# First layer's weights: the shift of the low word on ScalarE, the subtraction for the low part on VectorE

## The chip, the cores and the metric

The kernel runs on one core of a Trainium2 chip. The time is that of the device for one execution, in microseconds (us); less is better. The engines are named as in the profile: PE is TensorE's matmul, PEld its weight load, DVE is VectorE, ACT is ScalarE, POOL is GpSimd, SP is SyncE, which issues all the DMAs.

## The reference

Attention first: 4 batches, 8 heads of 64, 512 local and 32 global positions. Global queries see every key; a local query sees the global keys and the local ones within 32 positions of it. The result, 2176 tokens by 512, goes through two feed-forward layers, each with weights of its own (512 by 2048 and 2048 by 512):

```python
def _moe_ref(x, w_in, w_out):
    h = x @ w_in
    g = h * (1.0 / (1.0 + np.exp(-h)))
    return (g @ w_out).astype(np.float32)

def _moe2_ref(x, w_in, w_out):
    h = x @ w_in
    g = h * np.cos(h)
    return (g @ w_out).astype(np.float32)
```

Queries, keys and values are float32. The four weight matrices are float64, and they reach the chip as pairs of 32-bit words.

## The kernel before, in words

**Precision.** TensorE multiplies in a rounded float32 format (`F32R` in the code). So each operand is split into a high part, which is the value rounded to that format, and a low part, which is the value minus the high part. Each product is then three matmuls: low by high, high by high and high by low.

**Tiles and slots.** The tokens are cut into 8 tiles of 256 (the last has 384), the 2048 hidden units into 16 blocks of 128. A *slot* is one block of hidden units of one tile of tokens: `gemm1` (12 matmuls, L426 to L428) fills a PSUM tile `ps_hid`, ACT and DVE make the nonlinearity of it (`silu`, L434 and L435, in the first layer), `split_g` makes the two parts of the result (the cast `gh` on ACT, L406; the subtraction `gl`, L407, which is on POOL for the first layer's tiles 0 and 1 and on DVE elsewhere), and two slots later `gemm2` (12 matmuls, L493 to L495) adds it to the output tile `ps_y`. `ps_hid` has two buffers in the first layer, so `gemm1` of a slot waits for DVE's `silu` of the slot two before.

**Order.** The attention of tiles 0 and 1 comes before slot 0. Then the first layer's tiles 0 and 1 run with their slots in turn (slots 0 to 31), while the attention of tile 2 and the first global queries are spread between them. From slot 32 on the other tiles follow, then the second layer. Up to slot 40 the order of the instructions on every engine is left to the framework's scheduler, which sorts them by priority and by its own idea of when each is ready; from slot 40 it is the order written in the plan. Every engine works off its own queue in order.

**The first layer's weights.** They come as 32 chunks (`f` from 0 to 15, `part` 0 for `w_in`, 1 for `w_out`) of 128 rows by 512 float64 numbers, so 128 by 1024 words, and a chunk is needed at about one per slot. A chunk goes through these steps, planned in slots that follow one another:

- `load_w1` (SP, L99): one DMA of 512 KB into the tile `raw`, which has a buffer of its own for each chunk.
- `rebias` (ACT, L109): scales the high words, seen as float32, in place, which puts the exponent right.
- `to_f32` (DVE): shifts the low words right by 29, in place (L115); puts the sign bit of the high word to it (L116); shifts the high word left by 3 and joins the two (L120). The result is the chunk as float32, `w`, in a staging pool of three buffers that other tiles use too.
- `split_w`: the high part by a cast on ACT (L140), or on POOL for the first three chunks (L138, `POOLED`); the low part by a subtraction on POOL (L141). Both are written to `wt`, in the place where `raw` was.

The second layer's weights (`ph` of 1) are turned to float32 by the same functions in chunks of half the size, from slot 32 on, stored, and loaded and split when the second layer begins.

Of the kernel before, what the change touches and what calls it, by code (L numbers as in the profile page):

```python
# [11 lines left out]
F32 = mybir.dt.float32  # L12
F32R = mybir.dt.float32r
I32 = mybir.dt.int32
AF = mybir.ActivationFunctionType
ALU = mybir.AluOpType
PSUM = bass.MemoryType.PSUM
# [22 lines left out]
ROUND = 12582912.0  # L40
REBIAS = 2.0**-112
SIGN = -(2**31)


@with_exitstack
def attention_then_two_ffn(
# [9 lines left out]
    nc = tc.nc  # L56
# [32 lines left out]
    tiles = [(t, SPAN if t < NB - 1 else SPAN + B * SG) for t in range(NB)]  # L89
    x1 = [dram.tile([128, NP, n], F32, name=f"x1_{t}") for t, n in tiles]  # L90

# [1 line left out]
    w2f = [[dram.tile([128, 512], F32, name=f"w2f_{f}_{part}") for part in range(2)] for f in range(NF)]  # L93
    wh, wl = {}, {}
    W = {}

    def load_w1(f, part):
        raw = wts.tile([128, 1024], I32, tag=f"w{part}_{f}", name="raw")
        nc.sync.dma_start(out=raw, in_=w1[f, :, part * 1024 : part * 1024 + 1024])  # L99
        W[0, f, part] = raw.rearrange("p (n two) -> p n two", two=2)  # L100

    def load_w2_words(f, part):
        raw = stage.tile([128, 512], I32, tag="r", bufs=3, name="raw")
        nc.sync.dma_start(out=raw, in_=w2[f, :, part * 512 : part * 512 + 512])
        W[1, f, part] = raw.rearrange("p (n two) -> p n two", two=2)

    def rebias(ph, f, part):
        high = W[ph, f, part][:, :, 1].bitcast(F32)
        nc.scalar.activation(out=high, in_=high, func=AF.Copy, scale=REBIAS)  # L109

    def to_f32(ph, f, part):
        words = W[ph, f, part]
        n = words.shape[1]
        low, high = words[:, :, 0], words[:, :, 1]
        nc.vector.tensor_scalar(out=low, in0=low, scalar1=29, scalar2=None, op0=ALU.logical_shift_right)  # L115
        nc.vector.scalar_tensor_tensor(  # L116
            out=low, in0=high, scalar=SIGN, in1=low, op0=ALU.bitwise_and, op1=ALU.bitwise_or
        )
        w = stage.tile([128, n], F32, tag="f", name="w")
        nc.vector.scalar_tensor_tensor(  # L120
            out=w.bitcast(I32), in0=high, scalar=3, in1=low, op0=ALU.logical_shift_left, op1=ALU.bitwise_or
        )
        W[ph, f, part] = w
# [9 lines left out]
    def split_w(ph, f, part):  # L133
        w = W.pop((ph, f, part))
        t = wts.tile([128, 1024], F32R, tag=f"w{part}_{f}", name="wt")
        hi, lo = t[:, 0:512], t[:, 512:1024]
        if ph == 0 and 2 * f + part < POOLED:
            nc.gpsimd.tensor_scalar(out=hi, in0=w, scalar1=1.0, scalar2=1.0, op0=ALU.mult, op1=ALU.mult)  # L138
        else:
            nc.scalar.copy(hi, w)  # L140
        nc.gpsimd.tensor_tensor(out=lo, in0=w, in1=hi.bitcast(F32), op=ALU.subtract)  # L141
        wh[ph, f, part], wl[ph, f, part] = hi, lo

# [1 line left out]
    def attention_pools(stack):  # L145
        for name, bufs in (("qk", 2), ("v", 2), ("gin", 1), ("s", 2), ("t1", 1), ("st", 4)):
            P[name] = stack.enter_context(tc.tile_pool(name=name, bufs=bufs))

    # global values: rows hold [hi, lo, hi]; zeros between the two heads of a pair
    def load_vg(b):  # L150
        raw = stage.tile([128, DM], F32, tag="f", name="vraw")
        nc.sync.dma_start(out=raw[0:96], in_=vg3[b])
        t = P["t1"].tile([96, NP, 3, D], F32R, tag="vst", name="vst")
        nc.gpsimd.memset(t[:, :, 1, :].bitcast(F32), 0.0)
        vst[b] = t, raw
# [7 lines left out]
        )  # L163
        vst[b] = t.rearrange("r p h d -> r p (h d)")

    # P of the global keys, transposed: rows hold its parts [hi, hi, lo]
    def glob_keys_t(p, blocks):
        tg = P["t1"].tile([SG, blocks, 128], F32, tag="tg", name="tg")
        for g in range(4):
            rows = slice(32 * g, 32 * g + 32)  # L170
            nc.vector.transpose(out=tg[:, :, rows], in_=p[rows])
        return tg
# [5 lines left out]
        nc.gpsimd.tensor_tensor(out=pgt[64:96], in0=tg, in1=pgt[0:32].bitcast(F32), op=ALU.subtract)  # L178
        return pgt

    # local queries: four blocks of 64 queries, two heads each
    def load_qk(n):
        t = P["qk"].tile([128, QKCOLS], F32, tag="qk", name="qk")
        nc.sync.dma_start(out=t, in_=units[n, :, 0:QKCOLS])
        q = t[:, 0 : UNIT * 128].rearrange("p (c x) -> p c x", c=UNIT)
        k = t[:, UNIT * 128 : QKCOLS].rearrange("p (c x) -> p c x", c=UNIT)
        A[n] = {"q": q, "k": k}
# [31 lines left out]
    def unit_exp(n):  # L219
        s, st = A[n]["s"], A[n]["st"]  # L220
        for j in range(UNIT):
            nc.scalar.activation(
                out=s[:, j, :], in_=s[:, j, :], func=AF.Exp, bias=st[:, j : j + 1], scale=-1.0,
                accum_out=st[:, UNIT + j : UNIT + j + 1],
# [73 lines left out]
            nc.vector.tensor_tensor(out=lo, in0=po, in1=hi.bitcast(F32), op=ALU.subtract)  # L298
            A.pop(n)

    # global queries: 32 queries of four heads over all keys
    def load_glob_qk(n):
        t = P["gin"].tile([128, 2, 64 + KG], F32, tag="gin", name="gin")
        for i in range(2):
            nc.sync.dma_start(out=t[:, i, :], in_=glob[2 * n + i, :, 0 : 64 + KG])
        G[n] = {"qk": t}
# [27 lines left out]
    def glob_exp(n):  # L334
        st = G[n]["st"]
        G[n]["s"] = s = P["s"].tile([128, KG], F32, tag="s", name="sg")
        for c, ps in enumerate(G[n].pop("ps")):
            nc.scalar.activation(
                out=s[:, c * KG // 2 : (c + 1) * KG // 2], in_=ps, func=AF.Exp, bias=st[:, 2:3], scale=SCALE,
                accum_out=st[:, 3 + c : 4 + c],  # L340
# [54 lines left out]
            nc.vector.tensor_tensor(out=lo, in0=po, in1=hi.bitcast(F32), op=ALU.subtract)  # L395
            G.pop(n)

# [1 line left out]
    widest = [max(n for t, n in tiles if t % 3 == i) for i in range(3)]  # L399
    xbuf = [[xp.tile([128, NP, w], F32R, name=f"x{part}{i}") for part in "hl"] for i, w in enumerate(widest)]  # L400

# [29 lines left out]
    def silu(t, f):  # L431
        h = H.pop((0, t, f))
        a = M["a"].tile([128, tiles[t][1]], F32, tag="a", name="act")
        nc.scalar.activation(out=a, in_=h, func=AF.Tanh, scale=0.5)  # L434
        nc.vector.scalar_tensor_tensor(out=a, in0=a, scalar=1.0, in1=h, op0=ALU.add, op1=ALU.mult)  # L435
        g32[0, t, f] = a

    def turns(t, f):
# [3 lines left out]
        r = M["a"].tile([128, n], F32, tag="a", name="rest")  # L442
        nc.scalar.activation(out=k, in_=h, func=AF.Copy, scale=INV_TWO_PI, bias=ROUND)  # L443
        nc.vector.tensor_scalar(out=k, in0=k, scalar1=-ROUND, scalar2=None, op0=ALU.add)  # L444
# [4 lines left out]
    def load_sine():  # L449
        nc.scalar.activation(out=half_pi_sine, in_=half_pi, func=AF.Sin)  # L450

# [70 lines left out]
                r0 = t * SPAN + i * 128  # L522
                nc.sync.dma_start(out=out[r0 : r0 + 128, :], in_=o)

# [1 line left out]
    P, M, A, G, X1, H, Y, gq, g32, vst = ({} for _ in range(10))  # L526
    LAG = (2, 4)
    EARLY = 2 * NP
# [7 lines left out]
    last = (NB - 1) * NF  # L536
# [3 lines left out]
    def at(rank, i, fn, *args):  # L540
        plan.setdefault(i, []).append((rank, fn, args))
# [46 lines left out]
        if n + 1 < 2 * B:  # L588
            at(post, s + 5, load_glob_qk, n + 1)

    # attention of the first two tiles, then that of each later one during the tile before
    for n in range(2 * NP):
        plan_early_unit(n, n - LEAD)
    plan_glob(0, G0)
# [5 lines left out]
    for t in range(3, NB):  # L600
        s = (t - 1) * NF
# [7 lines left out]
        if t % 2 == 0:  # L609
            at(post, s - 2, load_vg, t // 2)  # L610
            at(pre, s + 2, split_vg, t // 2)
    # weights of the first layer
    chunks = sorted((seq.index((0, 0, f)) + LAG[0] * part, f, part) for f in range(NF) for part in range(2))
    s = len(seq)
    for need, f, part in reversed(chunks):
        s = max(min(s - 1, need - SLACK), 2 - LEAD)
        at(post, max(s - LOADS, 1 - LEAD), load_w1, f, part)
        at(pre, s, rebias, 0, f, part)
        at(pre, s + 1, to_f32, 0, f, part)
        at(pre, s + 2, split_w, 0, f, part)  # L620
    # weights of the second layer: to float32 meanwhile, to their place after the last use of the first's
    for i in range(4 * NF):
        s = PAIR + i * (last - PAIR - 4) // (4 * NF)
        at(post, s - 2, load_w2_words, i // 4, i % 4)
        at(pre, s, rebias, 1, i // 4, i % 4)
        at(pre, s + 1, to_f32, 1, i // 4, i % 4)
        at(pre, s + 1, store_w2, i // 4, i % 4)
    for f in range(NF):
        for part in range(2):
            s = last + f + 1 + part * LAG[0]  # L630
            at(post, s - 1, load_w2, f, part)
            at(pre, s, split_w, 1, f, part)
    # the two layers
    at(pre, last + NF, load_sine)
    for i, (ph, t, f) in enumerate(seq):
        at(pre, i + 1 + 2 * ph, split_g, ph, t, f)
# [8 lines left out]
    for t in range(NB):  # L645
        s = last + t * NF
# [97 lines left out]
```

## Time and profile before

| | |
|---|---|
| time, median of 3 runs | 947.88 us (947.23 to 948.92) |
| span of the profiled execution | 945.8 us |
| median less span, taken as what lies around the span | 2.1 us |
| PE busy | 908.6 us, 96% of the span |
| DVE busy | 666.3 us, 70% |
| ACT busy | 506.9 us, 54% |
| POOL busy | 185.9 us, 20% |
| chain that ended last | PE 86%, DVE 9%, DMA 2%, ACT 1% |

The profile is of one execution. Of the profiled execution its span is given; its own time is taken as the span and the 2.1 us beside it. Busy shares are means over a kernel whose parts differ: PE's 96% holds stretches with no idle time and one, early, in which it stands still again and again, so the shares have to be read by stretch.

### The profile page before, as it was taken

The page shows a single profiled execution, that of the slowest core. Times are in us where ns is not written, and L with a number is a line of the kernel's source. Part 1 is how long each engine was busy: PE and PEld are TensorE (multiplying, and loading weights), DVE is VectorE, ACT ScalarE, POOL GpSimd, SP SyncE. Part 2 cuts the span into 40 slices and gives each one's busy share as a digit, 9 for nine tenths or more (in the row PEclk, how much of TensorE's full clock was granted, in tenths as well). Part 3 has the DMA queues.
Part 4 walks back from the last instruction along what each step waited for, and adds up shares of the span by engine and source line. Part 5 has one row for each costly group of instructions (what it writes and reads, how often), then busy time and mean ns, then how long its engine had stood idle before and what let it go on. Part 6 is the DMA issues. An engine that isn't in the chain of part 4 may idle for free.

```text
span 945.8 us, 18534 instructions
## 1 busy us (share of the span) xinstructions
PE 908.6 (96%) x6800; PEld 851.0 (90%) x6800; DVE 666.3 (70%) x1873; ACT 506.9 (54%) x1386; POOL 185.9 (20%) x205
## 2 busy tenths in 40 slices
PE   6987889999999999999999999999999999999998
PEld 5676778999999999999999999999999999999997
DVE  5999995567686868778753557666666666676664
ACT  5655554445454545545445566565555555555543
POOL 2566664301111111110115650000000000000000
PEclk9998878999999999999999999999999999999999
DMA  8876421264464655656305440101010101010000
GB/s 284 301 246 221 167 93 37 74 206 158 157 218 147 193 184 158 190 164 192 116 29 167 128 140 2 45 1 45 1 46 1 45 1 45 2 56 1 23 1 33
DMA packets 48203, 102.12 MB, mean 108 GB/s; under 512 B 5361, under 2 KB 14065, under 8 KB 48113
## 3 DMA queue, kind: packets, MB, share of 16 engines
q1 hardware_dynamic: 48112, 100.95, 33.1%
q8 instruction: 53, 0.87, 0.4%
q14 instruction: 38, 0.30, 0.1%
HBM read 83.62 MB, written 17.30 MB: 107 GB/s over the span
## 4 chain that ended last, share of the span: by engine, by line
PE 86%; DVE 9%; DMA 2%; ACT 1%; issue 1%; SPq 0%; POOL 0%; ACTq 0%; DVEq 0%
PE ps_hid L428 13%; PE ps_hid L427 13%; PE ps_hid L426 13%; PE ps_y L493 7%; PE ps_y L500 7%; PE ps_y L499 7%; PE ps_y L501 7%; PE ps_y L495 6%; PE ps_y L494 6%; PE ps_s L200 3%; DVE w L120 2%; DVE raw L115 2%; DVE raw L116 2%; PE ps_o L286 2%; DMA raw<-in_w_dram 1%; PE ps_t L264 1%
## 5 line engine op out<-in xcount | busy, mean ns | idle before, releaser
L426 PE MATMUL ps_hid<-xh,wt 128*128 128x256 f32 (+1 forms) x1024 | 298.7, 292 | 10.2 <-DVE act L435 5.9
L427 PE MATMUL ps_hid<-xh,wt 128*128 128x256 f32 (+1 forms) x1024 | 298.1, 291 | 0.0
L428 PE MATMUL ps_hid<-xl,wt 128*128 128x256 f32 (+1 forms) x1024 | 298.1, 291 | 0.0
L426 PEld LDWEIGHTS ps_hid<-xh,wt 128*128 128x128 f32 x1024 | 197.6, 193 | 17.0 <-DVE act L435 6.5
L427 PEld LDWEIGHTS ps_hid<-xh,wt 128*128 128x128 f32 x1024 | 197.5, 193 | 4.9
L428 PEld LDWEIGHTS ps_hid<-xl,wt 128*128 128x128 f32 x1024 | 197.3, 193 | 0.0
L493 PE MATMUL ps_y<-gh,wt 128*128 128x256 f32 (+1 forms) x512 | 157.5, 308 | 0.0
L495 PE MATMUL ps_y<-gl,wt 128*128 128x256 f32 (+1 forms) x512 | 150.5, 294 | 0.5 <-POOL gl L407 0.5
L494 PE MATMUL ps_y<-gh,wt 128*128 128x256 f32 (+1 forms) x512 | 150.1, 293 | 0.0
L443 ACT ACTIVATE turns<-ps_hid 128x256 f32<-128x256 f32 (+1 forms) x128 | 50.8, 397 | 154.5 <-PE ps_hid L428 154.5
L444 DVE TENSOR_SCALAR turns<-turns 128x256 f32<-128x256 f32 (+1 forms) x128 | 38.7, 302 | 111.1 <-ACT turns L443 111.1
L500 PE MATMUL ps_y<-wt,gh 128*128 128x512 f32 x272 | 107.4, 395 | 0.0
L407 DVE TENSOR_TENSOR gl<-act,gh 128x256 fp32r<-128x256 f32 (+1 forms) x96 | 49.3, 513 | 82.4 <-ACT gh L406 82.2
L499 PE MATMUL ps_y<-wt,gl 128*128 128x512 f32 x272 | 107.2, 394 | 0.0
L501 PE MATMUL ps_y<-wt,gh 128*128 128x512 f32 x272 | 106.1, 390 | 0.0
L493 PEld LDWEIGHTS ps_y<-gh,wt 128*128 128x128 f32 x512 | 99.5, 194 | 4.6 <-issue 2.5
L495 PEld LDWEIGHTS ps_y<-gl,wt 128*128 128x128 f32 x512 | 99.7, 195 | 1.1 <-POOL gl L407 0.7
L494 PEld LDWEIGHTS ps_y<-gh,wt 128*128 128x128 f32 x512 | 99.9, 195 | 0.4 <-issue 0.4
L141 POOL TENSOR_TENSOR wt<-w,wt 128x512 fp32r<-128x512 f32 x64 | 89.8, 1415 | 51.8 <-ACT wt L140 46.6
L434 ACT ACTIVATE act<-ps_hid 128x256 f32<-128x256 f32 (+1 forms) x128 | 50.3, 393 | 53.8 <-PE ps_hid L428 52.7
L406 ACT CAST gh<-act 128x256 fp32r<-128x256 f32 (+1 forms) x128 | 52.9, 413 | 45.5 <-DVE act L435 22.0
L109 ACT ACTIVATE raw<-raw 128x256 f32<-128x256 f32 (+1 forms) x96 | 49.7, 519 | 51.0 <-DMA raw<-in_w_dram 50.9
(88 smaller groups left out, 1532.0 us busy)
## 6 DMA issues: line engine op xcount, KB each, us to landing
qk<-in_units_dram SPq DMA_DIRECT2D x32, 576.0 KB, 4.1
raw<-in_w_dram SPq DMA_DIRECT2D x32, 512.0 KB, 7.8
raw<-in_w_dram SPq DMA_DIRECT2D x64, 256.0 KB, 3.7
v<-in_units_dram SPq DMA_DIRECT2D x32, 256.0 KB, 3.0
w2f<-w SPq DMA_DIRECT2D x64, 128.0 KB, 1.8
w<-w2f SPq DMA_DIRECT2D x32, 256.0 KB, 2.6
gin<-in_glob_dram SPq DMA_DIRECT2D x16, 304.0 KB, 3.2
out_dram<-y SPq DMA_DIRECT2D x17, 256.0 KB, 2.1
```

The costliest lines, as they stand in the source:

```text
L141: nc.gpsimd.tensor_tensor(out=lo, in0=w, in1=hi.bitcast(F32), op=ALU.subtract)
L406: nc.scalar.copy(hi, src)
L426: nc.tensor.matmul(h, lo[:, ws], xh[:, k, :], start=k == 0, stop=False)
L427: nc.tensor.matmul(h, hi[:, ws], xh[:, k, :], start=False, stop=False)
L428: nc.tensor.matmul(h, hi[:, ws], xl[:, k, :], start=False, stop=k == NP - 1)
L443: nc.scalar.activation(out=k, in_=h, func=AF.Copy, scale=INV_TWO_PI, bias=ROUND)
L493: nc.tensor.matmul(o, lo[:, ds_], gh, start=first, stop=False, skip_group_check=True)
L494: nc.tensor.matmul(o, hi[:, ds_], gh, start=False, stop=False, skip_group_check=True)
L495: nc.tensor.matmul(o, hi[:, ds_], gl, start=False, stop=f == NF - 1, skip_group_check=True)
L499: nc.tensor.matmul(y[c], gl[:, cs], hi, start=f == 0, stop=False)
L500: nc.tensor.matmul(y[c], gh[:, cs], hi, start=False, stop=False)
L501: nc.tensor.matmul(y[c], gh[:, cs], lo, start=False, stop=f == NF - 1)
```

## The change

Three edits, all for the first layer's weights (`ph` of 0), and the two constants that one of them needs:

- `rebias` also does the shift of the low words, on ACT. A second activation reads the word as an unsigned integer, scales it by 2^-29 (a little less), adds a bias of almost -0.5, and writes it back as an integer, rounded, which gives the three bits that the shift gives.
- `to_f32` leaves out the shift on DVE (L115).
- `split_w` makes the low part on DVE, not on POOL (L141).

For the second layer's weights all stays as it was.

```diff
+U32 = mybir.dt.uint32
+TOP3 = 2.0**-29 * (1.0 - 2.0**-18)
+TOP3_BIAS = -0.5 + 7.5 * 2.0**-18
...
     def rebias(ph, f, part):
         high = W[ph, f, part][:, :, 1].bitcast(F32)
         nc.scalar.activation(out=high, in_=high, func=AF.Copy, scale=REBIAS)
+        if ph == 0:
+            low = W[ph, f, part][:, :, 0]
+            nc.scalar.activation(out=low, in_=low.bitcast(U32), func=AF.Copy, scale=TOP3, bias=TOP3_BIAS)
...
         low, high = words[:, :, 0], words[:, :, 1]
-        nc.vector.tensor_scalar(out=low, in0=low, scalar1=29, scalar2=None, op0=ALU.logical_shift_right)
+        if ph == 1:
+            nc.vector.tensor_scalar(out=low, in0=low, scalar1=29, scalar2=None, op0=ALU.logical_shift_right)
...
-        nc.gpsimd.tensor_tensor(out=lo, in0=w, in1=hi.bitcast(F32), op=ALU.subtract)
+        sub = nc.vector if ph == 0 else nc.gpsimd
+        sub.tensor_tensor(out=lo, in0=w, in1=hi.bitcast(F32), op=ALU.subtract)
```

## Rows read from the trace of the kernel before

**Rows 1.** Busy time of each engine by stretch (stretch, its length, then busy us)

```profile
core 0: us, PE busy (x) PEld busy (x) DVE busy (x) ACT busy (x) POOL busy (x), PEclk, DMA share, GB/s
...
25.00:43.00 18.00, 16.59 (x139) 12.18 (x139) 16.14 (x64) 12.75 (x43) 9.23 (x19) 1.00 0.89 298
43.00:150.00 107.00, 84.69 (x658) 79.53 (x654) 106.01 (x176) 57.31 (x138) 69.02 (x61) 0.89 0.53 178
150.00:190.00 40.00, 39.73 (x344) 38.98 (x345) 18.78 (x68) 18.16 (x56) 14.47 (x18) 0.96 0.18 57
...
230.00:500.00 270.00, 270.00 (x2496) 262.94 (x2496) 201.82 (x687) 135.62 (x422) 39.73 (x48) 1.00 0.51 160
```

**Rows 2.** Chain that ended last, 43 to 150 us, shares by line

```profile
by line: DVE w L120 19.8%; DVE raw L115 19.4%; DVE raw L116 17.8%; issue 10.0%; DMA raw<-in_w_dram 4.2%; DVE act L435 3.5%; DVE s L233 2.7%; DVE tg L171 2.5%; DVE sg L349 1.8%; DVE s L212 1.7%; DVE stg L329 1.4%; PE ps_y L495 1.2%; PE ps_y 
```

**Rows 3.** DVE's groups, 43 to 150 us (count, busy us, mean ns, idle before)

```profile
L116 DVE SCALAR_TENSOR_TENSOR raw<-raw 128x512 int32<-128x512 int32 x28 | 29.3, 1066 | 0.2
L115 DVE TENSOR_SCALAR raw<-raw 128x512 int32<-128x512 int32 x28 | 27.9, 1027 | 0.1
L120 DVE SCALAR_TENSOR_TENSOR w<-raw 128x512 int32<-128x512 int32 x28 | 24.7, 896 | 0.1
L435 DVE SCALAR_TENSOR_TENSOR act<-act,ps_hid 128x256 f32<-128x256 f32 x21 | 8.6, 408 | 0.0
L233 DVE TENSOR_SCALAR s<-s,st 128x160 f32<-128x160 f32 x8 | 5.6, 746 | 0.0
```

**Rows 4.** Timeline of DVE and of POOL, 79 to 86 us (start, length)

```profile
82.54 0.41 DVE L115 TENSOR_SCALAR raw<-raw 128x512 int32<-128x512 int32 x1
83.06 0.69 DVE L116 SCALAR_TENSOR_TENSOR raw<-raw 128x512 int32<-128x512 int32 x1
...
85.99 0.67 DVE L120 SCALAR_TENSOR_TENSOR w<-raw 128x512 int32<-128x512 int32 x1
...
81.14 0.93 POOL L407 TENSOR_TENSOR gl<-act,gh 128x256 fp32r<-128x256 f32 x1
84.65 0.74 POOL L407 TENSOR_TENSOR gl<-act,gh 128x256 fp32r<-128x256 f32 x1 [2.59 <-ACT gh L406]
```

**Rows 5.** Timeline of DVE and of POOL, 94 to 100 us

```profile
95.52 2.39 DVE L115 TENSOR_SCALAR raw<-raw 128x512 int32<-128x512 int32 x2
97.83 1.78 DVE L116 SCALAR_TENSOR_TENSOR raw<-raw 128x512 int32<-128x512 int32 x1
...
95.13 1.61 POOL L141 TENSOR_TENSOR wt<-w,wt 128x512 fp32r<-128x512 f32 x1
96.71 0.92 POOL L407 TENSOR_TENSOR gl<-act,gh 128x256 fp32r<-128x256 f32 x1
97.58 1.48 POOL L141 TENSOR_TENSOR wt<-w,wt 128x512 fp32r<-128x512 f32 x1
```

**Rows 6.** ACT's groups, 43 to 150 us

```profile
L140 ACT CAST wt<-w 128x512 fp32r<-128x512 f32 x29 | 17.7, 617 | 21.5 <-DVE w L120 21.3
L109 ACT ACTIVATE raw<-raw 128x512 f32<-128x512 f32 x26 | 17.5, 680 | 0.0
```

**Rows 7.** POOL's groups, 43 to 150 us

```profile
L141 POOL TENSOR_TENSOR wt<-w,wt 128x512 fp32r<-128x512 f32 x30 | 42.5, 1424 | 16.2 <-ACT wt L140 11.2 <-PE ps_y L495 1.9 <-issue 1.9
L407 POOL TENSOR_TENSOR gl<-act,gh 128x256 fp32r<-128x256 f32 x20 | 19.0, 952 | 19.9 <-ACT gh L406 12.6 <-PE ps_o L286 3.3 <-DMA raw<-in_w_dram 2.1
```

**Rows 8.** Waits, 43 to 150 us (us in total, times, longest)

```profile
ACT wt L140 <- DVE w L120: 21.3, 14, 3.4
ACT gh L406 <- DVE act L435: 13.6, 6, 3.8
...
POOL wt L141 <- ACT wt L140: 11.2, 6, 3.1
...
PE ps_hid L426 <- DVE act L435: 5.9, 3, 2.5
```

**Rows 9.** DVE's groups of the whole execution, for durations elsewhere

```profile
L233 DVE TENSOR_SCALAR s<-s,st 128x160 f32<-128x160 f32 x128 | 36.8, 348 | 0.8
...
L161 DVE TENSOR_TENSOR vst<-vraw,vst 32x512 fp32r<-32x512 f32 x4 | 2.7, 682 | 10.0 <-ACT vst L160 10.0
```

## The prediction, made before the change was run

> **What bounds the kernel now.** I read the busy time by stretch first, since the 96% of the whole hides where PE stands still. From 230 to 500 us PE is busy for all of 270.00 us and at full clock; nothing that DVE, ACT or POOL do there can shorten it. From 150 to 190 us it is busy 39.73 of 40.00. Between 43 and 150 us it is busy 84.69 of 107.00, idle for 22.3, while DVE is busy 106.01 of the 107.00 [rows 1]. So one stretch has an engine other than PE at its limit, and it is the one in which the first layer's weights are made. The chain agrees: its three largest lines there are DVE's three steps of a weight chunk, 57% together [rows 2], and the waits show DVE as the one waited for by ACT (21.3 us for a finished chunk, 13.6 for the nonlinearity) and by PE [rows 8]. ACT is busy 57.31 us and POOL 69.02 of 107: both have room [rows 1].
>
> The stretch also has a granted clock of 0.89, against 1.00 later [rows 1]: PE ran partly at 1.2 instead of 2.4 GHz in it, in a stretch in which it stopped again and again. At full clock its 84.69 us would be some 75 (84.69 x 0.89, an estimate). The most that can be won is therefore about 107 - 75 = 32 us. Ahead of 43 us PE is busy 16.59 of 18.00 and the DMA engines 0.89 of the time [rows 1], so I expect nothing there from the few chunks that are made so early.
>
> Why DVE is full is the next question. Its 28 shifts L115 cost 1027 ns each, L116 1066, L120 896 [rows 3]. But while POOL stands still, from 82.07 to 84.65 us, L115 takes 0.41 and L116 0.69, and after 85.39 L120 takes 0.67 [rows 4]. Where POOL's L141 and L407 follow one another, two L115 take 2.39 and one L116 1.78 [rows 5]. L435, which has an operand in PSUM, keeps 408 ns throughout [rows 3]. So POOL's work holds up those DVE instructions that work in SBUF alone, and POOL's work is 42.5 us of L141 in 69.02 [rows 7, 1].
>
> **The change part by part**, for the stretch of 43 to 150 us.
>
> 1. *L115 leaves DVE.* 28 x 1027 ns: 27.9 us off [rows 3]. The few of earlier chunks lie under PE and the loads, and count as nothing; were that cover gone, 4 more would add some 2 us by the undisturbed 0.41.
>
> 2. *The subtraction comes to DVE.* No such row of 128x512 exists; the nearest is the same operation over the same 512 columns, L161, at 682 ns [rows 9]. POOL has made 30 in the stretch [rows 7], DVE will make some 29: 29 x 0.682 = 19.8 us on. At an undisturbed L120's 0.67 it would be 19.4, at a disturbed one's mean of 896 ns 26.0.
>
> 3. *POOL's L141 goes, and with it a part of the holding up.* What L116, L120 and L233 lose now: 29.3 - 28 x 0.68 = 10.3; 24.7 - 28 x 0.67 = 5.9; 5.6 - 8 x 0.348 = 2.8 (0.348 is the mean of the whole run); 19.0 in all [rows 3, 4, 9]. POOL keeps 69.02 - 42.5 = 26.5 us; in a stretch of some 91 us that is a share of 0.29, against 0.645 now, so 0.45 of the loss would stay and 10.4 go. The subtraction is itself an operation with both inputs in SBUF, like L116 and L120. These lose (10.3 + 5.9) / 56 = 0.29 us each now, so it would lose 0.13, 29 times: 3.8 on. Bounds: the whole 19.0 goes and the subtraction loses nothing; or none of it goes and the subtraction loses the full 0.29, 8.4 us.
>
> The Trainium skill (SBUF — State Buffer, Who interferes with whom) says that VectorE instructions with two SBUF inputs contend with GpSimd instructions that read SBUF, by an exclusive lock. By that rule the new subtraction queues behind what POOL keeps too, and the trace agrees as far as L116's 1.78 us against 0.69 and L435's steady 408 ns go. [...]
>
> 4. *The second activation comes to ACT.* Nearest is L109, in place on the same strides, at 680 ns; the cast L140, without strides, takes 617 [rows 6]. Neither has an integer on both sides, so the price is open; I take 680, as the strides are the same. 28 x 0.68 = 19.0 us on ACT: 57.3 + 19.0 = 76.3 of some 91 us. It costs nothing because ACT stands idle for 49.7 us of the stretch, 21.3 of them waiting for DVE's chunks [rows 1, 8]. DVE's first step of a chunk waits for ACT's rebias already, and now for one activation more; the loads run ahead, so I count nothing. If ACT's cover were gone, up to 19 us would return.
>
> 5. *A new wait.* DVE's subtraction needs ACT's cast. POOL now waits for that cast 11.2 us in all, 6 times, up to 3.1 [rows 8], which holds up nobody but the next `gl`; on DVE the same wait would hold up L435 (so `ps_hid`, so `gemm1`) and every step of the next chunk. But 21.3 us of ACT's own waits are for DVE, and they shrink when DVE is faster. I count 1 us, with 0 and 11.2 as bounds. For three chunks the high part is POOL's (L138), before or just after 43 us; nothing counted. The staging buffer of `w` comes free when DVE is done, not POOL; nothing counted.
>
> 6. *PE's clock.* With fewer stops I expect part of the low clock to go. While DVE is the limit this gives nothing; just after 150 us the mean of 0.96 over 40 us [rows 1] is worth 1.6 us. I take that off.
>
> Sum: -27.9 + 19.8 - 10.4 + 3.8 + 1 - 1.6 = -15.3 us; the stretch falls from 107 to some 92. DVE is still the limit then, with ACT at 76 and PE at some 75 to 80 close behind. After the stretch PE is at work all the time, so a gain there reaches the end undiminished. The profiled execution has a span of 945.8 and 2.1 around it; its sum, 947.9, is the median of the runs. Forecast: 947.9 - 15.3 = 932.6, **932.6 us**.
>
> **The rivals.**
>
> *Full relief.* L141 is the one whose removal counts: what POOL keeps is short pieces that fall beside DVE's PSUM work. Then -27.9 + 19.8 - 19.0 - 1.6 = -28.7, close to PE's own 32: **919 us**, bounded by PE and ACT. For it: L407 took 0.74 alone, L141 1.42 in the mean [rows 4, 7]. Against: three engines within a few us of one another in queues worked off in order never fit without gaps.
>
> *Two engines in each other's way (smaller gain).* ACT is filled and DVE waits for the cast as POOL does now, 11.2 instead of 1 us: -15.3 + 10.2 = -5: **943 us**. The same comes of an integer activation that takes 1.05 us: 10 us more on ACT, and it stands at 86 of 92, with tanh and cast queued behind. For it: every chunk would pass ACT, DVE, ACT, DVE. Against: ACT's idle time.
>
> *No change.* No relief, and the subtraction suffers as L120 does: -27.9 + 19.8 + 8.4 = +0.3: **948 us**. It needs POOL's remaining 26.5 us to do the harm of its 69.
>
> *Slower.* The subtraction at the head of DVE's queue waits for a cast that stands behind activations waiting for PE or for a load. The gain is 16.3 without the wait; over 29 chunks the point is 0.56 us each. At the longest of today's waits for a cast, 3.1, six stalls make 19, and at 0.8 us each for all 29 it is 23: -16.3 + 23 = +7, **955 us**. For it: the scheduler orders the queues by its own idea of when things are ready, up to slot 40, and a new order may put the subtraction too early. Against: the mean wait over today's 30 is 11.2 / 30 = 0.37.
>
> **How the numbers follow.** Chances: the forecast (gain of 9 to 21) 0.60; full relief (over 21) 0.17; smaller gain (2 to 9) 0.13; no change 0.03; slower 0.07. A measurement of this kernel can tell about 0.2%, 1.9 us, from no change. Faster by more than that: 0.60 + 0.17 + 0.13 = 0.90; within it 0.03; slower 0.07. For the range I take the forecast's case, most of full relief and most of the smaller gain: 920 to 943 (gains of 28 to 5). Outside it stay the slower and unchanged cases (0.10), a third of the smaller gain (0.04) and some of full relief (0.04).
>
> **What would show it.** In the changed profile: DVE still above 95% busy through the weights, but ending near 135 us instead of 150; L116 and L120 with means of 0.75 to 0.85 us; the subtraction near 0.7 to 0.85; POOL below a third; ACT's second activation near 0.68 and ACT at some 80% there; PE idle for less than 15 us of the stretch and fewer spells of low clock. I am wrong if DVE shows idle time before the subtraction (a wait for L140) of over 10 us, if the activation takes more than 1 us, if L116 and L120 stay near 1 us, or if ACT's queue, and with it PE, waits for loads.

## The result, and the profile after

The changed kernel takes 925.11 us (median of 4 runs, 924.26 to 926.57) beside 948.30 for the kernel before in the same job: ratio 0.9756, 95% interval 0.9743 to 0.9770. That is 23 us less, where 15.3 were forecast; 925.1 lies inside the range of 920 to 943, between the forecast's own 932.6 and the rival of full relief (919), and a little nearer to the rival.

Busy time by stretch, of the changed kernel, answers to [rows 1]:

```profile
core 0: us, PE busy (x) PEld busy (x) DVE busy (x) ACT busy (x) POOL busy (x), PEclk, DMA share, GB/s
25.00:43.00 18.00, 16.04 (x143) 12.46 (x142) 16.49 (x74) 15.59 (x50) 7.08 (x18) 1.00 0.89 287
43.00:150.00 107.00, 99.55 (x872) 93.70 (x871) 100.71 (x229) 83.03 (x206) 41.98 (x42) 0.98 0.59 201
150.00:190.00 40.00, 39.45 (x340) 37.66 (x339) 22.47 (x77) 19.10 (x57) 8.91 (x12) 1.00 0.47 138
230.00:500.00 270.00, 270.00 (x2398) 263.36 (x2398) 198.30 (x649) 136.28 (x411) 51.63 (x53) 1.00 0.52 158
```

In the same 107 us PE now stands idle for 7.45 us instead of 22.3, and its clock is 0.98 instead of 0.89. DVE falls to 100.71, ACT rises from 57.31 to 83.03, POOL falls from 69.02 to 41.98. From 230 to 500 us PE is full in both kernels.

DVE's groups from 43 to 150 us (count, busy us, mean ns, idle before), for [rows 3]. The numbers of the lines have moved: L124 was L116, L128 was L120, L150 is the subtraction, L444 was L435.

```profile
L128 DVE SCALAR_TENSOR_TENSOR w<-raw 128x512 int32<-128x512 int32 x29 | 24.1, 830 | 0.1
L150 DVE TENSOR_TENSOR wt<-w,wt 128x512 fp32r<-128x512 f32 x31 | 24.1, 777 | 0.1
L124 DVE SCALAR_TENSOR_TENSOR raw<-raw 128x512 int32<-128x512 int32 x29 | 22.2, 781 | 0.0
L444 DVE SCALAR_TENSOR_TENSOR act<-act,ps_hid 128x256 f32<-128x256 f32 x27 | 11.0, 409 | 2.5 <-ACT act L443 2.3
```

A chunk costs DVE 0.83 + 0.78 + 0.78 = 2.39 us, where it cost 1.07 + 1.03 + 0.90 = 2.99. The subtraction waits for nothing: 0.1 us of idle time before 31 of them. L444, with its operand in PSUM, keeps its 409 ns.

ACT's groups, for [rows 6], with the new activation L116:

```profile
L116 ACT ACTIVATE raw<-raw 128x512 int32<-128x512 uint32 x27 | 18.4, 682 | 0.0
L148 ACT CAST wt<-w 128x512 fp32r<-128x512 f32 x29 | 18.0, 620 | 7.9 <-DVE w L128 7.9
L113 ACT ACTIVATE raw<-raw 128x512 f32<-128x512 f32 x26 | 17.9, 687 | 0.6 <-DMA raw<-in_w_dram 0.6
```

With integers on both sides the activation takes what the float one on the same strides takes, 682 and 687 ns. ACT's wait for DVE's chunk has gone from 21.3 [rows 8] to 7.9 us.

POOL's largest group, for [rows 7]; L416 was L407:

```profile
L416 POOL TENSOR_TENSOR gl<-act,gh 128x256 fp32r<-128x256 f32 x26 | 28.4, 1094 | 52.0 <-ACT gh L415 48.0 <-PE ps_y L504 1.6 <-PE ps_sg L330 1.6
```

Waits from 43 to 150 us, for [rows 8]:

```profile
ACT wt L148 <- DVE w L128: 7.9, 10, 1.8
ACT gh L415 <- DVE act L444: 4.3, 4, 2.8
...
DVE act L444 <- ACT act L443: 2.3, 2, 1.3
```

To see where the time was won I follow PE's slots: four `gemm1` matmuls with `lo` open the four quarters of a slot, so the first of every fourth one marks a slot's start. These are the starts of slots 0, 22 and 40 in PE's timeline, first of the kernel before, then of the changed one:

```profile
43.68 0.36 PE L426 MATMUL ps_hid<-xh,wt 128*128 128x256 f32 x1
...
154.34 0.28 PE L426 MATMUL ps_hid<-xh,wt 128*128 128x256 f32 x1
...
221.06 0.28 PE L426 MATMUL ps_hid<-xh,wt 128*128 128x256 f32 x1
```

```profile
49.05 0.36 PE L435 MATMUL ps_hid<-xh,wt 128*128 128x256 f32 x1
...
131.11 0.28 PE L435 MATMUL ps_hid<-xh,wt 128*128 128x256 f32 x1
...
198.87 0.28 PE L435 MATMUL ps_hid<-xh,wt 128*128 128x256 f32 x1
```

Slot 0 begins 5.4 us later than before. Slots 0 to 22 take 82.1 us instead of 110.7, so 28.6 less; slots 22 to 40 take 67.8 instead of 66.7. Together: 5.4 - 28.6 + 1.1 = -22.1, which is the whole difference of the spans (945.8 and 923.7); what comes after slot 40 is the same to 0.1 us. So the change won more than its result shows, and lost a part of it before slot 0.

What was lost there has two parts. PE's 260 matmuls ahead of slot 0 keep it busy for 36.9 us instead of 33.4, and it is idle for 12.2 instead of 10.2. The longer busy time goes with the clock: in the first 25 us its mean was 0.93 before and is 0.80 now (first the row of the kernel before):

```profile
0.00:25.00 25.00, 16.16 (x118) 13.70 (x119) 14.44 (x72) 14.28 (x47) 6.79 (x25) 0.93 0.83 286
0.00:25.00 25.00, 16.62 (x86) 13.17 (x87) 9.59 (x51) 11.60 (x38) 5.59 (x21) 0.80 0.69 241
```

Two more figures by slot are used below: how many chunks DVE has joined when slot 22 starts (32 before, 31 in the changed kernel), and the time of DVE's steps on chunks between slots 0 and 22, summed from the start of each instruction to its end or to the next one's start (77.2 us before, 57.8 now).

### The profile page after: what moved, and what is told of

It is laid out like the page before. It is cut to its first block, busy times and chain, and to the rows that moved or that the text cites. A ratio compares the mean times of both kernels' runs of the same rounds, so it can differ in the third digit from the quotient of the medians.

```text
span 923.7 us, 18475 instructions
## 1 busy us (share of the span) xinstructions
PE 901.7 (98%) x6800; PEld 843.6 (91%) x6800; DVE 646.9 (70%) x1873; ACT 522.6 (57%) x1418; POOL 149.9 (16%) x173
## 4 chain that ended last, share of the span: by engine, by line
PE 86%; DVE 9%; ACT 2%; DMA 2%; issue 1%; POOL 1%; SPq 0%; ACTq 0%; POOLq 0%
PE ps_hid L437 13%; PE ps_hid L436 13%; PE ps_hid L435 13%; PE ps_y L509 7%; PE ps_y L508 7%; PE ps_y L510 7%; PE ps_y L502 6%; PE ps_y L504 6%; PE ps_y L503 6%; PE ps_s L209 3%; DVE w L128 2%; PE ps_o L295 2%; DVE wt L150 2%; DMA raw<-in_w_dram 2%; DVE raw L124 2%; PE ps_t L273 1%
## 5 line engine op out<-in xcount | busy, mean ns | idle before, releaser
L435 PE MATMUL ps_hid<-xh,wt 128*128 128x256 f32 (+1 forms) x1024 | 296.5, 290 | 0.2 <-DVE act L444 0.2
L435 PEld LDWEIGHTS ps_hid<-xh,wt 128*128 128x128 f32 x1024 | 195.7, 191 | 6.2 <-DVE act L444 0.7
L502 PE MATMUL ps_y<-gh,wt 128*128 128x256 f32 (+1 forms) x512 | 155.7, 304 | 0.2 <-ACT gh L415 0.2
L503 PE MATMUL ps_y<-gh,wt 128*128 128x256 f32 (+1 forms) x512 | 148.5, 290 | 0.0
L416 DVE TENSOR_TENSOR gl<-act,gh 128x256 fp32r<-128x256 f32 (+1 forms) x96 | 51.2, 533 | 82.1 <-ACT gh L415 81.4
L502 PEld LDWEIGHTS ps_y<-gh,wt 128*128 128x128 f32 x512 | 97.9, 191 | 5.0 <-issue 2.1
L503 PEld LDWEIGHTS ps_y<-gh,wt 128*128 128x128 f32 x512 | 98.2, 192 | 0.4 <-issue 0.4
L444 DVE SCALAR_TENSOR_TENSOR act<-act,ps_hid 128x256 f32<-128x256 f32 (+1 forms) x128 | 55.1, 430 | 23.5 <-ACT act L443 23.3
L415 ACT CAST gh<-act 128x256 fp32r<-128x256 f32 (+1 forms) x128 | 52.9, 413 | 29.5 <-DVE act L444 15.3
```

The costliest lines, as they stand in the source:

```text
L415: nc.scalar.copy(hi, src)
L416: engine.tensor_tensor(out=lo, in0=src, in1=hi.bitcast(F32), op=ALU.subtract)
L435: nc.tensor.matmul(h, lo[:, ws], xh[:, k, :], start=k == 0, stop=False)
L502: nc.tensor.matmul(o, lo[:, ds_], gh, start=first, stop=False, skip_group_check=True)
L503: nc.tensor.matmul(o, hi[:, ds_], gh, start=False, stop=False, skip_group_check=True)
```

## The experiments

Theory A is that what was won is mostly the time for which POOL held up DVE, whoever of DVE's instructions it met. Theory B is that it is mostly the shift's own cost, which left DVE. All times beside their baseline runs in the same job (947.65, 948.12 and 948.72 us in the three jobs).

**One part alone.** The first run moves only the shift, the second only the subtraction.

```diff
-        sub = nc.vector if ph == 0 else nc.gpsimd
-        sub.tensor_tensor(out=lo, in0=w, in1=hi.bitcast(F32), op=ALU.subtract)
+        nc.gpsimd.tensor_tensor(out=lo, in0=w, in1=hi.bitcast(F32), op=ALU.subtract)
```

> The shift is ACT's, the subtraction stays POOL's. Theory A (what POOL holds up goes with POOL's busy time, whichever DVE instruction it meets): before, DVE lost some 37 us of the stretch (16.3 on L115, 19.0 on L116, L120 and L233, the rest on others) to POOL's 69 us, 0.53 us for each; all of it stays, and only L115's own 28 x 0.41 = 11.5 us are saved: about 936 us, L124 and L128 at means over 1.1 us. Theory B (each instruction's loss is its own, so L115's 27.9 us go as a whole): DVE needs 78 us, PE becomes the limit, 919 to 925 us, L124 and L128 at about 1.0.

Measured: 943.63 us, ratio 0.9962 (0.9950 to 0.9975). DVE's and POOL's groups from 43 to 150 us, where L128 and L124 are the two steps left to DVE:

```profile
L128 DVE SCALAR_TENSOR_TENSOR w<-raw 128x512 int32<-128x512 int32 x29 | 33.4, 1153 | 3.2 <-POOL wt L149 2.1
L124 DVE SCALAR_TENSOR_TENSOR raw<-raw 128x512 int32<-128x512 int32 x29 | 28.1, 974 | 3.4 <-ACT raw L116 3.1
...
L149 POOL TENSOR_TENSOR wt<-w,wt 128x512 fp32r<-128x512 f32 x30 | 44.6, 1493 | 11.5 <-ACT wt L148 10.6 <-PE ps_s L208 0.5
```

All shifts of the first layer have left DVE, 27.9 us in [rows 3], and the kernel gains 4 us. Slot 0 starts at 50.4 us here, 6.7 later than before; slots 0 to 22 take 97.9 us instead of 110.7, 12.7 less, about the 11.5 that theory A allows the shift. So A, which forecast 936 and is too hopeful by 8, misses by the late start in the main. Theory B (919 to 925) falls, even with 6.7 us added.

But A does not hold as a whole. L128 became slower, 1153 ns against 896 in [rows 3], as A has it; L124 at 974 stayed under the 1.1 us that A expects. Between slots 0 and 22 the shift's 26.7 us are off and the two joins take 4.8 more, so only a part of what POOL had held up in the shift came back in them. DVE also stands idle for 9.5 us there, where it was 1.8, and it is no longer full:

```profile
43.00:150.00 107.00, 90.92 (x730) 82.80 (x729) 94.88 (x171) 74.93 (x180) 74.19 (x64) 0.91 0.56 189
```

Its largest waits from 43 to 150 us are for ACT's new activation (3.1 us), for PE (2.7) and for POOL's L149 (2.1). Whether they too come of POOL's subtraction is not shown.

```diff
-        if ph == 0:
-            low = W[ph, f, part][:, :, 0]
-            nc.scalar.activation(out=low, in_=low.bitcast(U32), func=AF.Copy, scale=TOP3, bias=TOP3_BIAS)
...
-        if ph == 1:
+        if True:
             nc.vector.tensor_scalar(out=low, in0=low, scalar1=29, scalar2=None, op0=ALU.logical_shift_right)
```

> The subtraction is DVE's, the shift stays DVE's. Theory A: the loss falls to 26.5 x 0.53 = 14 us, the subtraction adds 19.8: 106 - 37 + 14 + 19.8 = 103 us, about 945 us, the shift at a mean of 0.5 to 0.65. Theory B: the subtraction adds 19.8 and only a part of 19.0 goes: 106 + 19.8 - 10 = 116 us, about 957 us.

Measured: 928.13 us, ratio 0.9789 (0.9774 to 0.9804). DVE's groups from 43 to 150 us (L120 is the shift, L121 and L125 the two joins, L147 the subtraction):

```profile
L121 DVE SCALAR_TENSOR_TENSOR raw<-raw 128x512 int32<-128x512 int32 x28 | 22.7, 809 | 0.0
L125 DVE SCALAR_TENSOR_TENSOR w<-raw 128x512 int32<-128x512 int32 x29 | 22.4, 771 | 0.0
L147 DVE TENSOR_TENSOR wt<-w,wt 128x512 fp32r<-128x512 f32 x28 | 22.3, 798 | 0.5 <-POOL wt L143 0.5
L120 DVE TENSOR_SCALAR raw<-raw 128x512 int32<-128x512 int32 x29 | 15.6, 551 | 0.1
```

DVE has one more instruction for each chunk, and the kernel is 19.5 us faster. The shift, at the same place as before, costs 551 instead of 1027 ns. A chunk takes 2.93 us of DVE with four steps, less than the 2.99 it took with three: the subtraction adds 0.80, and the other three are 0.86 shorter. B expected a loss and falls again. Theory A had the direction and under-rated it (945 expected, 928 measured).

The chunk's cost does not explain that much: 0.06 us on 29 chunks are 1.7 us. The rest goes along with another order. When slot 22 starts, DVE has joined 25 chunks here, where it had joined 32 before. Slots 0 to 22 take 83.9 us instead of 110.7, and slots 22 to 40, into which the seven chunks moved, 72.1 instead of 66.7. So this run shows that DVE's other steps get shorter when POOL's subtraction goes, but its time is not the price of that alone; how much the order won is not separated here.

The two parts give 4.0 and 19.5 us by themselves, 23.5 in sum, and 23.2 together. That they add up is chance: between slots 0 and 22 they win 12.7, 26.8 and together 28.6 us, and each run starts slot 0 at another time.

**POOL's work put back.** In the changed kernel POOL makes the subtraction a second time, which nobody needs.

```diff
         sub.tensor_tensor(out=lo, in0=w, in1=hi.bitcast(F32), op=ALU.subtract)
+        if ph == 0:
+            nc.gpsimd.tensor_tensor(out=lo, in0=w, in1=hi.bitcast(F32), op=ALU.subtract)
```

> The changed kernel, in which POOL makes the subtraction once more after DVE, to the same place (work without use). If what POOL holds up was the larger part of the gain, DVE's three instructions of a chunk go from 0.78 to 0.85 us to over 1.0 us each and the time to 940 to 950 us. If the gain is ACT's taking of the shift alone, it stays within 5 us of 925.

Measured: 948.40 us, ratio 1.0007 (0.9995 to 1.0019): the whole gain is gone. Groups from 43 to 150 us:

```profile
L150 DVE TENSOR_TENSOR wt<-w,wt 128x512 fp32r<-128x512 f32 x27 | 29.9, 1106 | 0.0
L124 DVE SCALAR_TENSOR_TENSOR raw<-raw 128x512 int32<-128x512 int32 x27 | 29.6, 1109 | 0.0
L128 DVE SCALAR_TENSOR_TENSOR w<-raw 128x512 int32<-128x512 int32 x27 | 26.0, 964 | 1.2 <-POOL wt L152 1.2
...
L152 POOL TENSOR_TENSOR wt<-w,wt 128x512 fp32r<-128x512 f32 x27 | 41.3, 1531 | 17.8 <-DVE wt L150 14.5 <-ACT wt L148 2.4 <-POOL pgt L188 0.7
```

DVE's steps are at 0.96 to 1.11 us each, at the same work as in the changed kernel. A part of the loss could lie in `lo` being ready later, but the 0.79 us that each chunk costs DVE more (3.18 against 2.39) is 21 us over 27 chunks. The order is no rival here: when slot 22 starts, DVE has joined 31 chunks in both kernels. Slots 0 to 22 take 106.0 us instead of 82.1, 23.9 more, and 21.7 of that are DVE's steps on chunks (79.5 against 57.8).

**Is it POOL's reading?** Instead of a second subtraction POOL does two needless operations ahead of DVE's: two copies of `w`, or two memsets, each to the place of `lo`.

```diff
         hi, lo = t[:, 0:512], t[:, 512:1024]
+        if ph == 0:
+            for _ in range(2):
+                nc.gpsimd.tensor_scalar(out=lo, in0=w, scalar1=1.0, scalar2=1.0, op0=ALU.mult, op1=ALU.mult)
```

> The changed kernel, with two needless copies of w to the place of the low part on POOL before each chunk's subtraction (one input each; 0.62 us each by the row of L138's like, so 1.24 us a chunk against the 1.42 of the subtraction that was there). If POOL's reading of SBUF is what holds DVE up: the three DVE steps at 0.95 to 1.1 us, the time 940 to 950 us. If it needs two inputs on POOL's side: means as in the changed kernel and a time within 5 us of 925, but for what the subtraction waits for the copies.

```diff
+                nc.gpsimd.memset(lo.bitcast(F32), 0.0)
```

> The same with two needless memsets in the place of the two copies, so that POOL is busy about as long and writes the same bytes, but reads nothing. If it is the reading: the three DVE steps at their 0.78 to 0.83 us and a time within 5 us of 925. If POOL's busy time as such, or its writing, is what holds DVE up: as with the copies, 940 to 950 us.

Measured: 944.52 us with the copies, ratio 0.9957 (0.9940 to 0.9973), and 928.42 with the memsets, ratio 0.9791 (0.9774 to 0.9808). Groups from 43 to 150 us with the copies, then with the memsets; L153 is the subtraction, L147 POOL's needless work:

```profile
L153 DVE TENSOR_TENSOR wt<-w,wt 128x512 fp32r<-128x512 f32 x29 | 27.5, 949 | 5.4 <-POOL wt L147 5.1
L124 DVE SCALAR_TENSOR_TENSOR raw<-raw 128x512 int32<-128x512 int32 x28 | 26.3, 958 | 0.0
L128 DVE SCALAR_TENSOR_TENSOR w<-raw 128x512 int32<-128x512 int32 x28 | 23.8, 849 | 0.1
...
L147 POOL TENSOR_SCALAR wt<-w 128x512 fp32r<-128x512 f32 x58 | 51.5, 890 | 17.9 <-DVE w L128 13.8 <-POOL pgt L190 0.7 <-ACT pt L280 0.7
```

```profile
L128 DVE SCALAR_TENSOR_TENSOR w<-raw 128x512 int32<-128x512 int32 x30 | 24.5, 818 | 0.1
L153 DVE TENSOR_TENSOR wt<-w,wt 128x512 fp32r<-128x512 f32 x31 | 24.4, 788 | 2.7 <-POOL wt L147 2.7
L124 DVE SCALAR_TENSOR_TENSOR raw<-raw 128x512 int32<-128x512 int32 x29 | 23.2, 818 | 0.0
...
L147 POOL MEMSET wt<- 128x512 f32 x60 | 31.5, 528 | 19.5 <-DVE w L128 15.9 <-POOL pgt L190 1.3 <-ACT s L234 0.7
```

With 31.5 us of memsets DVE's steps stay at 0.79 to 0.82 us, as in the changed kernel. It is not that POOL was idle: it is busy for 70.26 us of the stretch, as much as in the kernel before (69.02):

```profile
43.00:150.00 107.00, 97.63 (x835) 90.55 (x832) 100.34 (x221) 81.88 (x201) 70.26 (x103) 0.98 0.57 194
```

With copies DVE's steps go to 0.85 to 0.96, somewhat under the 0.95 to 1.1 expected, and the copies themselves take 890 ns each, half again the 0.62 expected of them. So POOL has to read SBUF to hold DVE up; two inputs are not needed. The memsets' run is 3 us slower than the changed kernel, and its subtraction waits 2.7 us for them. In both runs 31 chunks are joined when slot 22 starts. Slots 0 to 22 take 99.2 us with the copies and 85.5 with the memsets, against 82.1. Of the copies' 17.1 us, 10.4 are longer steps on chunks; 4.4 are more idle time of DVE, the subtraction's wait for the copies above all, which is another harm than the holding up. The Trainium skill (SBUF — State Buffer, Who interferes with whom) says just this of VectorE instructions with two SBUF inputs: they contend with a GpSimd instruction that reads SBUF, not with one that only writes it. The two runs agree: 0.85 to 0.96 us with the copies, 0.79 to 0.82 with the memsets.

**What POOL still does.** `gl` of tiles 0 and 1 goes to DVE too, first in the changed kernel.

```diff
-        split(hi, lo, g32.pop((ph, t, f)), nc.gpsimd if ph == 0 and t < 2 else nc.vector)
+        split(hi, lo, g32.pop((ph, t, f)), nc.vector)
```

> The changed kernel with gl of tiles 0 and 1 on DVE too, so that POOL has almost nothing left in the stretch. If what POOL still does (28.4 us of gl from 43 to 150) is what keeps DVE's three steps of a chunk at 0.78 to 0.83 us, they fall to 0.68 to 0.70, which gives back some 10 us, while gl costs DVE 26 x 0.41 = 10.7: within 3 us of 925. If those means have another cause they stay, and the time rises by up to 10 us.

Measured: 922.51 us, ratio 0.9733 (0.9714 to 0.9751). Groups from 43 to 150 us:

```profile
L150 DVE TENSOR_TENSOR wt<-w,wt 128x512 fp32r<-128x512 f32 x30 | 21.6, 722 | 1.3 <-ACT wt L148 1.2
L128 DVE SCALAR_TENSOR_TENSOR w<-raw 128x512 int32<-128x512 int32 x29 | 19.8, 682 | 0.1
L124 DVE SCALAR_TENSOR_TENSOR raw<-raw 128x512 int32<-128x512 int32 x28 | 19.5, 698 | 0.1
L416 DVE TENSOR_TENSOR gl<-act,gh 128x256 fp32r<-128x256 f32 x28 | 13.8, 494 | 0.5 <-ACT gh L415 0.5
```

The means fall to what they are beside an idle POOL [rows 4], so POOL's remaining reads were what kept them at 0.78 to 0.83. DVE has 28 more instructions and PE is busy for 103.40 us of the stretch instead of 99.55. The three steps give back 9.5 us (70.4 to 60.9, with two instructions fewer), and `gl` costs 13.8, at 494 ns each more than the 10.7 expected; the order helped too, since DVE has joined 27 chunks when slot 22 starts, not 31. The gain of 2.6 us on the changed kernel is at the edge of the two intervals, and slot 0 starts 2.2 us earlier here (46.88 us), which the edit touches only through the scheduler's order.

**The late start.** All three edits undone for the first three chunks, then the shift alone undone for them.

```diff
-        if ph == 0:
+        if ph == 0 and 2 * f + part >= POOLED:
             low = W[ph, f, part][:, :, 0]
...
-        if ph == 1:
+        if ph == 1 or 2 * f + part < POOLED:
             nc.vector.tensor_scalar(out=low, in0=low, scalar1=29, scalar2=None, op0=ALU.logical_shift_right)
...
-        sub = nc.vector if ph == 0 else nc.gpsimd
+        sub = nc.vector if ph == 0 and 2 * f + part >= POOLED else nc.gpsimd
```

> The change for all chunks but the first three (those whose high part is POOL's). In the changed kernel slot 0 begins at 49.0 us, 5.3 later than before. If the three early chunks' new steps are the cause: slot 0 at 43 to 45 us, about 920 us. If it is the order or PE's clock in the first 25 us: slot 0 at 47 to 50 us, 924 to 927 us.

The second run has the first two hunks only.

> The changed kernel, with only the shift of the first three chunks back on DVE; their subtraction stays DVE's. If ACT's three early activations are what made slot 0 late, it begins at 45 to 46 us and the time is 920 to 922 us. If it was the subtraction's wait for POOL's high part at the head of DVE's queue, slot 0 stays at 48 to 50 us and the time at 924 to 926 us.

Measured: 921.18 us with all undone, ratio 0.9714 (0.9699 to 0.9728), and 923.93 with the shift alone undone, ratio 0.9747 (0.9731 to 0.9762). Slot 0 of the one, then of the other:

```profile
45.28 0.36 PE L435 MATMUL ps_hid<-xh,wt 128*128 128x256 f32 x1
```

```profile
46.56 0.36 PE L435 MATMUL ps_hid<-xh,wt 128*128 128x256 f32 x1
```

With the early chunks on the old path 3.8 of the 5.4 us come back at slot 0, and 3.9 in the time. Giving back the shift alone brings slot 0 forward by 2.5 us, but the time by 1.2, which the intervals do not tell from nothing: the reading there was mixed. So three chunks' new steps delay the start, the shift on ACT with some part in it. The other runs point the same way: slot 0 starts at 50.39 us with the shift alone moved and at 46.05 with the subtraction alone, against 43.68 before. How much is the order that the scheduler then chose stays open, as it can't be held fixed from the kernel's text; it is worth some 2 us at least, for the run with `gl` on DVE has the changed kernel's early chunks and starts slot 0 at 46.88.

**What limits next.** The step that joins the sign is left out in the changed kernel.

```diff
-        nc.vector.scalar_tensor_tensor(
-            out=low, in0=high, scalar=SIGN, in1=low, op0=ALU.bitwise_and, op1=ALU.bitwise_or
-        )
+        if ph == 1:
+            nc.vector.scalar_tensor_tensor(
+                out=low, in0=high, scalar=SIGN, in1=low, op0=ALU.bitwise_and, op1=ALU.bitwise_or
+            )
```

> The changed kernel without the step that joins the sign to the low word of the first layer's weights, so all these weights come out positive: a look at what the time would be with less on DVE. It takes 29 x 0.78 = 22.6 us off DVE in the stretch. If DVE is still the limit there and PE close behind, the time falls by the 5 to 7 us that PE is idle from 43 to 150 us: 917 to 921 us. If ACT or PE is the limit already, it stays within 2 us of 925. Were DVE the only limit, with PE far behind, it would fall by 15 us or more.

Measured: 919.10 us, ratio 0.9696 (0.9681 to 0.9711): a third of DVE's work on the weights removed, and 6 us won. Busy time by stretch, then DVE's group of the nonlinearity:

```profile
43.00:150.00 107.00, 103.12 (x925) 98.33 (x926) 81.15 (x201) 83.82 (x207) 38.72 (x45) 1.00 0.59 200
...
L445 DVE SCALAR_TENSOR_TENSOR act<-act,ps_hid 128x256 f32<-128x256 f32 x29 | 11.9, 411 | 11.8 <-ACT act L444 11.8
```

Now DVE waits for ACT's activation of PE's result, 11.8 us, and PE is busy 103.12 of 107. In the changed kernel DVE was still the limit, with PE about 6 us behind.

**The two that helped, together.** The early chunks on the old path, and `gl` on DVE.

> The change for all chunks but the first three, and gl of tiles 0 and 1 on DVE. If the two edits do not meet (the one acts before slot 0, the other after), the time is that of the kernel with the first edit alone, 921.2, plus what the second gives by itself: 918 to 924 us.

Measured: 917.75 us (917.20 to 918.19), ratio 0.9686 (0.9670 to 0.9702): faster than both kernels, and as fast as the kernel with a third of the chunk work left out. By themselves the edits gave 3.9 and 2.6 us on the changed kernel, and together 7.4. For `gl` on DVE this run beside the one with the first three chunks undone is the cleaner comparison, as slot 0 starts at 45.2 and 45.3 us: 917.75 against 921.18, 3.4 us less, outside both intervals. Busy time by stretch:

```profile
43.00:150.00 107.00, 103.18 (x916) 99.00 (x917) 100.81 (x258) 83.31 (x207) 13.07 (x17) 1.00 0.56 190
```

PE stands idle for 3.8 us of the stretch at full clock. There is little left to win in it.

## Why the prediction was right, and where it was off

- *The bound* was read rightly. The gain lies between slots 0 and 22, where DVE was full and still is: it stands idle for 1.8 us there before and 2.5 now. PE is the limit behind it, and what comes after slot 40 did not move.

- *Steps 1 to 3 as a mechanism*: right, and shown by the runs that put POOL's work back, with and without reading. The means came as forecast: 0.78 and 0.83 for the joins (0.75 to 0.85 forecast), 0.78 for the subtraction (0.7 to 0.85). But the amounts were booked in the wrong place. The sum took the shift's 27.9 us as won when it leaves DVE, and 10.4 for relief. The run with the shift alone won 12.7 us between slots 0 and 22, not 27.9, and 4 in the time. Beside a silent POOL the shift takes 0.41 us, and in the run with the subtraction alone it took 0.55: most of its 1.03 was POOL's doing. Step 3 counted the loss of three other lines and left out the largest, the shift's own 16.4 us (27.9 - 28 x 0.41), which stands under step 1. As both edits were made at once, that did not spoil the sum.

- *How much of the loss stays*: the forecast's 0.45 was luck. The joins lost 0.58 us a chunk before and lose 0.25 now, so 0.43 stayed. But the forecast took the loss to follow POOL's share of the stretch, and that share is 0.39, not 0.29; by its own rule 0.61 would have stayed. What POOL keeps does less harm for its time than L141 did, which is the thought of the full-relief rival, though not so far as it went: the run with `gl` on DVE still won some 0.1 us on each join. One reading for that rival was wrong too. L407's 0.74 us were not "alone": L120 began 0.04 us later and took 1.25 instead of 0.67.

```profile
84.69 1.25 DVE L120 SCALAR_TENSOR_TENSOR w<-raw 128x512 int32<-128x512 int32 x1
```

- *The size*: forecast -15.3, measured -23.2 (-22.1 between the two profiled executions). By the prediction's own bands a gain over 21 belongs to full relief (chance 0.17) and not to its case of 9 to 21. One account is PE's, from the two pages. PE does the same 6800 matmuls; its busy time fell from 908.6 to 901.7 us (6.9) and its idle time from 37.2 to 22.0 (15.2), 22.1 in all, the difference of the spans. By slots, the busy time fell by 11.2 us between slots 0 and 22 (88.1 to 76.9 for the same 680 matmuls), where the clock rose, and grew by 3.5 ahead of slot 0, where it fell. Step 6 gave the clock 1.6. But this account tells where PE's time went and not what set it: with DVE the limit, the size is to be looked for in DVE's terms.

- The other account is DVE's. For the stretch the forecast has -13.7 without step 6, and slots 0 to 22 became 28.6 shorter. I summed, from slot 0 to slot 22, the time from each of DVE's instructions to its end or the next one's start. The chunk steps account for 19.4 of the 28.6 us: the shift 26.65 off, the joins from 50.58 to 39.22, the subtraction 18.61 on. The forecast has 13.2 for the same lines (27.9 + 8.9 - 23.6). So the terms most in error are the subtraction, 5.0 us cheaper than forecast, and the joins' relief, 2.5 larger; that one chunk less falls between these slots (27 instead of 28) makes some 2 us of both. Another 10 us are three kinds: the attention's L233 (6.7 to 1.7, where step 3 gave it 1.5 of relief; four of its twelve instructions fall elsewhere now), the first steps of three chunks of the second layer's weights, which no longer fall among these slots (3.8), and L349 (2.0 to 0.8). The scheduler's new order took some of these out of the stretch. The two accounts describe the same 22 us from two sides and are not to be added.

- *Inside the range, with luck*: the stretch won twice what was forecast for it, and 6.5 us were lost outside it (5.4 before slot 0, 1.1 from slot 22 to 40), where the forecast had 1.6 won. The two errors have opposite signs. Without the late start the time would be about 919.7 (925.1 - 5.4), just under the range.

- *The chunks before 43 us, counted at nothing*, were not nothing: slot 0 came 5.4 us later. Where the sum said "under PE and the loads" it had looked at the two engines that the chunks leave, not at the one that they come to: the early attention passes through ACT, and the chunks' second activation with it. That this is the way is argued, not shown. ACT was not full (11.60 of the first 25 us, 15.59 of the next 18), and PE's lower clock in the first 25 us and the scheduler's order have a part that no run separates.

- *Step 4*: right, 682 ns against 680, ACT at 83.0 of 107 us (78%; 80% forecast). *Step 5*: the feared wait did not come, 0.1 us before the subtraction where 1 was counted. So the slower rival and that of two engines in each other's way fell by the same row, the latter's other branch (an activation of 1.05 us) by the 682 ns.

- *What would show it*: DVE is 94% busy (over 95% forecast); its last step on these weights ends at 140.8 us, not near 135, after a start that came 5.4 late. POOL is 39% busy (under a third forecast), since 26 `gl` fall in the stretch instead of 20 and each grew from 952 to 1094 ns. PE's idle time of 7.45 us is under the 15 named.

## What to carry to other kernels

An instruction that is slow in a stretch may only be the one that meets the neighbour: before counting its mean as won, compare it with its own shortest time, and do not count the rest as won before it is clear who holds it up. Moving work from POOL to a DVE that is already full can pay: here the subtraction cost DVE 0.80 us a chunk, and its three other steps became 0.86 us shorter. Where a scheduler sets the order, compare kernels by slots and count what each has done by then: an edit can win or lose time through the order alone. And when a step moves to an engine with room, look at that engine's room at the start too, not only in the stretch that the change is for.

## What the runs showed that was not expected

- A DVE busy for 94% of the stretch took on 28 more instructions (13.8 us of `gl`) and the kernel got no slower (925.1 to 922.5 us): 9.5 us came back as POOL fell almost silent, and four chunks moved behind slot 22.
- POOL's reads are slowed in return: the copy of 128x512 took 890 ns in the mean where three of them took 621 before, `gl` 1094 ns where it took 740 when it began ahead of DVE's L120 [rows 4]. Memsets of the same size took 528 ns and lengthened none of DVE's steps on chunks.
- From 43 to 150 us the low clock went almost wholly with PE's stops: a mean of 0.89 before, 0.98 after, 1.00 with the best version. In the first 25 us it did not: 0.93, 0.80 and 0.86.
